# Attention with a gated MLP on one core: instructions recorded first and placed by a planner, chunk 0 by quarter tiles, early attention with tokens on partitions

## The chip, the core and the metric

The kernel runs on one core of a Trainium2 chip. Five engines take part, each with an instruction stream that it works through in order: TensorE (PE, with its weight loads as PEld), VectorE (DVE), ScalarE (ACT), GpSimd (POOL, hardly used here) and SyncE (SP), which issues the DMAs. Matmuls write to PSUM; everything else lives in SBUF or in DRAM. The metric is the device time of one launch in microseconds.

## The reference

```python
# x: 8 batches, 8 heads, 512 tokens, 64; state: 8 batches, 8 heads, 32 states, 64
scores = scale * x @ state.T;  a = softmax(scores)     # over the 32 states
xread  = a @ state                                     # 512 rows for each batch
scores2 = scale * state @ x.T; a2 = softmax(scores2)   # over the 512 tokens
sread  = a2 @ x                                        # 32 rows for each batch
X = concat([xread, sread]), heads side by side         # 4608 x 512
out = ((X @ w_a) * (X @ w_b)) @ w_out                  # 512 -> 1536 -> 512
```

All is float32.

## The kernel before

**Precision.** Float32 values are split into two parts of a shorter format, fp32r, high and low (`_h`, `_l`), and a product is made of three matmuls: high by high, low by high, high by low. The weights come as 64-bit words and are converted on the chip: class `Conv` loads one tile (`raw`), ScalarE scales it (`pre`), VectorE takes six operations of 512 columns (`run`), ScalarE writes the halves.

**Algebra.** xread is never formed. Since xread @ W = a @ (state @ W), the states are first multiplied into the weights. The 1536 columns of w_a and w_b are cut into six chunks (`c`) of 256 columns of each. For a chunk, `project` multiplies states (`sd_h`, `sd_l`) by weights (`wq`) for four batches at a time (`bg`), ScalarE copies the products to `sw_st` (or to `wo10`, `wo11`), and two DMAs for each pair of heads store them to DRAM (`scr`). `Batch.load` reads them back in another layout, one tile `p_raw` for a batch and a chunk, and `split` makes `p_h` (ScalarE) and `p_l` (VectorE). This store and load is called a round trip below, and the split tile a piece. Two pieces take a direct way (`DIRECT`): batch 0 with chunk 0 and batch 2 with chunk 1 get their products by small fp32 matmuls with the batch's own states (`direct`).

**Attention.** `Attention` handles one batch `b` and half of the heads `g`. `scores` puts states on partitions and tokens along the rows; `soft` takes the maxima over tokens, and VectorE's stream transpose turns 32x32 blocks so that the states lie along the rows for the other softmax (`s_p`); `exp`, `norm`; `back` turns the result again (`a_tr`) and splits it into `at_h`, `at_l`. `reads`, `sread` and `keep` make the 32 rows of sread with matmuls.

**MLP.** `layer1` of a step takes a batch and a block of 128 columns (`ft`): twice six matmuls of 512 columns from `p_h`, `p_l` and `at_h`, `at_l` into `ab`, then ScalarE copies, VectorE multiplies, and `g_h`, `g_l` are split. `layer2` of a step, which comes `LAG` = 2 steps later, adds twelve matmuls into `acc`. `VISITS` lists which batch takes which chunks, in order. A batch that comes back fetches its partial sums.

**Order.** The steps carry lists: `sp` and `pre` before layer 1, `fill` between the matmuls of layer 2, `post` behind it. Tables of step numbers (`ATTEND`, `CONV`, `CONVO`, `CONVS`) and a hand-written list `begin` say where each load, conversion, product and piece of attention goes. The framework's own scheduler then places the instructions within that.

Of the kernel before, what the change touches and what calls it, by code (L numbers as in the profile page):

```python
# [49 lines left out]
def attn_moe(ctx, tc, xt, xn, sd, wl, w_out, out):  # L50
    nc = tc.nc

    const = ctx.enter_context(tc.tile_pool(name="const", bufs=1))
    proj = ctx.enter_context(tc.tile_pool(name="proj", bufs=2))
    att = ctx.enter_context(tc.tile_pool(name="att", bufs=2))
    mlp = ctx.enter_context(tc.tile_pool(name="mlp", bufs=2))
    dram = ctx.enter_context(tc.tile_pool(name="dram", bufs=1, space=bass.MemoryType.DRAM))
    ps_acc = ctx.enter_context(tc.tile_pool(name="ps_acc", bufs=4, space=bass.MemoryType.PSUM))
    ps_ab = ctx.enter_context(tc.tile_pool(name="ps_ab", bufs=2, space=bass.MemoryType.PSUM))
    ps_ms = ctx.enter_context(tc.tile_pool(name="ps_ms", bufs=2, space=bass.MemoryType.PSUM))  # L60
# [7 lines left out]
    ident = const.tile([P, P], F32, name="ident")  # L68
    make_identity(nc, ident)
# [91 lines left out]
    def project(c, hp, bg, hh, psp, tag):  # L161
        if hh == 0:
            name, bufs = SW[st["n"] % len(SW)]
            st[bg], st["n"] = proj.tile([P, 2, 512], F32, name=name, bufs=bufs), st["n"] + 1
        sw = st[bg]
        ps = psp.tile([P, 512], F32, name=tag)
        for k, s in enumerate((sd_h, sd_l)):
            nc.tensor.matmul(ps, lhsT=s[hp // 2][:, 2 * (hp % 2) + hh, bg], rhs=w[c, hp][:, hh],  # L168
                             start=(k == 0), stop=(k == 1))
# [23 lines left out]
    class Attention:  # L193
# [5 lines left out]
        def load(self):  # L199
            self.x = att.tile([P, 2, S + D], F32, name="x_raw", bufs=1)  # L200
            nc.sync.dma_start(out=self.x, in_=xt[self.b, self.g])

        def scores(self):

            self.s = ps_ms.tile([P, 512], F32, name="ms")
            for hp in range(2):
                nc.tensor.matmul(self.s[hp * D:(hp + 1) * D], lhsT=self.x[:, hp, S:S + D],  # L207
                                 rhs=self.x[:, hp, :S], start=True, stop=True)

        def soft(self):  # L210
# [17 lines left out]
        def norm(self):  # L228
            sp, m1, m2 = self.sp, self.m1, self.m2
# [6 lines left out]
            nc.vector.tensor_scalar_add(out=m2[:, 3:4], in0=m2[:, 2:3], scalar1=EPS)  # L236
            nc.vector.reciprocal(out=m2[:, 3:4], in_=m2[:, 3:4])
# [8 lines left out]
        def reads(self):  # L246
            ps = ps_ms.tile([P, 512], F32, name="ms")
            for sb in range(4):
                nc.tensor.transpose(ps[:, sb * P:(sb + 1) * P], self.e2[:, sb * P:(sb + 1) * P], ident)  # L249
            self.a2 = att.tile([P, 4, P], F32, name="a2", bufs=1)  # L250
            nc.scalar.copy(out=self.a2.rearrange("p a b -> p (a b)"), in_=ps)
# [8 lines left out]
        def sread(self):  # L260

            ps = self.s = ps_ms.tile([P, 512], F32, name="ms")
            for sb in range(4):
                for hp in range(2):
                    nc.tensor.matmul(ps[hp * D:(hp + 1) * D, :P],  # L265
                                     lhsT=self.a2[:, sb, hp * D:(hp + 1) * D],
                                     rhs=self.xn[:, sb, hp * P:(hp + 1) * P],
                                     start=(sb == 0), stop=(sb == 3))
            nc.scalar.mul(out=self.a2[:, 0, :], in_=ps[:, :P], mul=self.m2[:, 3:4])
# [22 lines left out]
    class Batch:  # L292
# [20 lines left out]
        def direct(self, c, g, psp, tag, srcs):  # L313

            if g == 0:
                self.new_piece(c)
            ps = psp.tile([P, 512], F32, name=tag)
            for i, s in enumerate(srcs):
                for hq in range(4):
                    nc.tensor.matmul(ps[hq * NS:(hq + 1) * NS], lhsT=s(hq), rhs=f32(w[c, 2 * g + hq // 2][:, hq % 2]),  # L320
                                     start=(i == 0), stop=(i == len(srcs) - 1))
# [85 lines left out]

    def layer1(u, ft):
        res = []
        for ab in range(2):  # L410
            ps = ps_ab.tile([P, 512], F32, name="ab")
            m = 0
            for k in range(u.nk):
                xh, xl = u.rhs(k)
                wh, wlo = u.lhs(ft, k, ab)
                for a, b in ((wh, xh), (wh, xl), (wlo, xh)):
                    nc.tensor.matmul(ps[:, :u.n], lhsT=a, rhs=b, start=(m == 0), stop=(m == 3 * u.nk - 1))  # L417
# [11 lines left out]
    def layer2(u, ft, first, last, final, g, fill=()):  # L429
# [5 lines left out]
        for i in range(nt):  # L435
# [3 lines left out]
            for k, (l, r) in enumerate(((gh, 0), (gh, 1), (gl, 0))):  # L439
                nc.tensor.matmul(u.acc[i], lhsT=l[:, ts], rhs=wo[ft][:, r],  # L440
                                 start=(first and k == 0), stop=(last and k == 2))
# [10 lines left out]


    sp, pre, fill, post = ([[] for _ in steps] for _ in range(4))

    def at(where, n, f, *args):
        where[n].append(lambda: f(*args))

    queue = sorted([(n, 0, c, hp) for c, ns in CONV.items() for hp, n in enumerate(ns)] +
                   [(n, 1, ft, 0) for ft, n in CONVO.items()] +
                   [(n + j, 2, ft, j) for ft, n in CONVS.items() for j in range(2)])
    first = [(-1, 0, 0, hp) for hp in range(4)] + [(-1, 1, ft, 0) for ft in range(2)]
    queue = first + queue
    make = conv_w, lambda ft, _: conv_o(ft), units[SU].conv
    convs = [make[k](a, b) for _, k, a, b in queue]
    early = max(i for i, x in enumerate(queue) if x[0] < 35)
    late = min(i for i, x in enumerate(queue) if x[1] == 2)
    loads = []  # L470
    for i, c in enumerate(convs):
# [5 lines left out]
        loads.append((i + 1 - len(ring), c, ring[i % len(ring)]))
    done = [0]

    def next_load(n=1):  # L480

        done[0] += n
        while loads and loads[0][0] <= done[0]:
            _, c, place = loads.pop(0)
            c.load(place)
# [5 lines left out]


    a0, a1, a2 = [[atts[b, g] for g in range(2)] for b in range(3)]
    c0 = convs[:6]
    u0, u1, u2 = units[:3]

    def projects(c, hp, bg, psp=ps_acc, tag="acc"):
        for hh in range(2):
            project(c, hp, bg, hh, psp, tag)

    done[0] = -3
    begin = [next_load, a0[0].load, lambda: next_load(2), load_states, lambda: new_a(0),
             c0[0].pre, c0[0].run, a0[0].scores, next_load, a0[0].soft, a0[1].load, a0[0].nat,
             c0[1].pre, lambda: states(0, 0), c0[1].run, next_load, a0[0].exp, a0[0].norm, a0[1].scores,
             a1[0].load, c0[2].pre, lambda: u0.direct0(0, 0), a0[0].reads, a0[1].soft, a0[0].back,
             c0[2].run, next_load, lambda: states(1, 0), a0[1].exp, a0[1].norm, c0[3].pre,
# [136 lines left out]
```

## Time and profile before

| | |
|---|---|
| median of 3 runs | 756.52 us (756.07 to 756.76) |
| profiled execution | 758.62 us, of it span 756.8 us |
| TensorE busy | 711.0 us, 94% of the span |
| VectorE busy | 492.2 us, 65% |
| ScalarE busy | 392.6 us, 52% |
| mean granted clock of TensorE | 0.977 |
| moved by DMA | 134.30 MB, mean 177 GB/s |

Busy time counts an instruction from its start to its end; consecutive instructions of an engine overlap in their pipelines, so the distance of two starts is shorter than the duration of one. A row of a window gives, for each engine, the busy time and the number of instructions in it; an fp32 matmul leaves two records. The chain that ended last is followed back from the last instruction, at each step to what released it.

### The profile page before, as it was taken

How to read it: one execution, taken by the hardware profiler on the slowest of the kernel's cores; microseconds unless marked ns; L12 is line 12 of the kernel's file. 1: busy time of each engine (PE TensorE's matmuls, PEld its weight loads, DVE VectorE, ACT ScalarE, POOL GpSimd, SP SyncE). 2: the span in 40 equal slices, each digit the busy share in tenths (PEclk: the TensorE clock that was granted, in tenths of full speed). 3: DMA queues.
4: the chain of work that ended last, by engine and by line, in shares of the span. 5: the costliest groups of instructions: out<-in, count | busy, mean ns of one | idle time of the engine just before them, and what ended most of it. 6: DMA issues, size and time to landing. Idle time of an engine off the chain costs nothing.

```text
span 756.8 us, 9364 instructions
## 1 busy us (share of the span) xinstructions
PE 711.0 (94%) x3304; PEld 549.6 (73%) x3304; DVE 492.2 (65%) x961; ACT 392.6 (52%) x712; POOL 0.7 (0%) x6
## 2 busy tenths in 40 slices
PE   3759997999899999997999999999999999999997
PEld 0326765787577788885777777788889888888887
DVE  6989875887788754735899847463339823695232
ACT  5857848766786456755454424333236523553221
POOL 0000000000000000000000000000000000000000
PEclk9989999899899999998999999999999999999999
DMA  8795965947959573558888623121116311420002
GB/s 312 248 326 173 313 226 195 393 182 262 317 209 320 220 249 125 196 195 285 294 294 267 239 84 111 56 94 45 57 56 195 117 51 56 152 71 29 0 1 84
DMA packets 54798, 134.30 MB, mean 177 GB/s; under 512 B 5088, under 2 KB 5088, under 8 KB 54752
## 3 DMA queue, kind: packets, MB, share of 16 engines
q1 hardware_dynamic: 54464, 132.67, 50.7%
q10 hardware_dynamic: 288, 1.05, 0.4%
q8 instruction: 26, 0.43, 0.2%
q14 instruction: 20, 0.16, 0.1%
HBM read 87.03 MB, written 46.66 MB: 177 GB/s over the span
## 4 chain that ended last, share of the span: by engine, by line
PE 87%; DMA 5%; ACT 4%; DVE 2%; issue 1%; DVEq 0%; SPq 0%; ACTq 0%
PE ab L417 40%; PE acc L440 36%; PE ms L168 4%; PE ms L265 2%; DMA p_raw<-scr 2%; PE ms L207 2%; DMA scr<-wo 1%; PE ms L249 1%; DMA scr<-sw_st 1%; ACT wo L170 1%; DMA raw<-wl 1%; ACT sw_st L170 1%; ACT t L96 1%; DVE sd_l L66 1%; PE acc L320 1%
## 5 line engine op out<-in xcount | busy, mean ns | idle before, releaser
L440 PE MATMUL acc<-wo,g_h 128*128 128x512 f32 x816 | 232.8, 396 | 1.3 <-ACT g_h L425 1.3
L440 PEld LDWEIGHTS acc<-wo,g_h 128*128 128x128 f32 x816 | 151.9, 188 | 38.4 <-ACT g_h L425 1.7
L422 DVE TENSOR_TENSOR a_sb<-ab,a_sb 128x512 f32<-128x512 f32 (+1 forms) x108 | 71.3, 660 | 163.4 <-PE ab L417 158.2
L417 PE MATMUL ab<-at_h,p_h 128*128 128x512 f32 x384 | 157.0, 411 | 10.5 <-ACT at_h L243 5.5
L417 PE MATMUL ab<-at_l,p_h 128*128 128x512 f32 x384 | 155.2, 404 | 0.0
L417 PE MATMUL ab<-at_h,p_l 128*128 128x512 f32 x384 | 153.0, 401 | 0.0
L440 PE MATMUL acc<-wo,g_l 128*128 128x512 f32 x408 | 137.6, 398 | 0.0
L421 ACT COPY a_sb<-ab 128x512 f32<-128x512 f32 (+1 forms) x108 | 60.9, 564 | 140.7 <-PE ab L417 139.4
L425 ACT CAST g_h<-a_sb 128x512 fp32r<-128x512 f32 (+1 forms) x108 | 64.4, 596 | 72.6 <-DVE a_sb L422 72.3
L417 PEld LDWEIGHTS ab<-at_h,p_h 128*128 128x128 f32 x384 | 74.0, 193 | 35.7 <-ACT at_h L243 6.1
L440 PEld LDWEIGHTS acc<-wo,g_l 128*128 128x128 f32 x408 | 76.0, 188 | 18.8 <-DVE t L109 0.8
L417 PEld LDWEIGHTS ab<-at_l,p_h 128*128 128x128 f32 x384 | 74.6, 194 | 18.2 <-DVE m L236 1.6
L417 PEld LDWEIGHTS ab<-at_h,p_l 128*128 128x128 f32 x384 | 73.5, 192 | 18.1 <-DVE t L111 0.9
L66 DVE TENSOR_TENSOR g_l<-a_sb,g_h 128x512 fp32r<-128x512 f32 (+1 forms) x108 | 71.1, 658 | 22.7 <-ACT g_h L425 22.4
L310 ACT CAST p_h<-p_raw 128x512 fp32r<-128x512 f32 x92 | 52.4, 618 | 49.8 <-PE ab L417 40.3
L66 DVE TENSOR_TENSOR p_l<-p_raw,p_h 128x512 fp32r<-128x512 f32 x92 | 60.2, 683 | 7.5 <-ACT p_h L310 7.5
L102 DVE TENSOR_SCALAR t<-t 128x512 int32<-128x512 int32 x60 | 25.2, 423 | 31.0 <-ACT t L96 16.3
L168 PE MATMUL ms<-wq,sd_h 128*128 128x512 f32 x88 | 35.8, 407 | 4.9 <-ACT sw_st L170 4.6
L168 PE MATMUL ms<-wq,sd_l 128*128 128x512 f32 x88 | 35.1, 399 | 0.0
L170 ACT COPY sw_st<-ms 128x512 f32<-128x512 f32 x44 | 25.6, 589 | 15.3 <-PE ms L168 14.9
L207 PE MATMUL ms<-x_raw 128*64 128x512 f32 x64 | 19.2, 682 | 15.1 <-DMA x_raw<-xt 11.3
L170 ACT COPY wo<-ms 128x512 f32<-128x512 f32 x44 | 25.3, 589 | 11.0 <-PE ms L168 10.8
(98 smaller groups left out, 745.9 us busy)
## 6 DMA issues: line engine op xcount, KB each, us to landing
p_raw<-scr SPq DMA_DIRECT2D x46, 512.0 KB, 3.9
scr<-sw_st SPq DMA_DIRECT2D x48, 256.0 KB, 3.4
scr<-wo SPq DMA_DIRECT2D x48, 256.0 KB, 4.0
raw<-wl SPq DMA_DIRECT2D x21, 512.0 KB, 5.6
part<-stg SPq DMA_DIRECT2D x20, 512.0 KB, 4.1
stg<-part SPq DMA_DIRECT2D x20, 512.0 KB, 6.0
x_raw<-xt SPq DMA_DIRECT2D x16, 576.0 KB, 5.4
out<-stg SPq DMA_DIRECT2D x34, 256.0 KB, 3.8
```

The source lines that it names most:

```text
L66: eng.tensor_tensor(out=out, in0=in0, in1=in1, op=ALU.subtract)
L102: nc.vector.tensor_scalar(out=t2, in0=t1, scalar1=3, scalar2=0x7FFFF000, op0=ALU.logical_shift_left, op1=ALU.bitwise_and)
L168: nc.tensor.matmul(ps, lhsT=s[hp // 2][:, 2 * (hp % 2) + hh, bg], rhs=w[c, hp][:, hh], start=(k == 0), stop=(k == 1))
L170: nc.scalar.copy(out=sw[:, hh], in_=ps)
L207: nc.tensor.matmul(self.s[hp * D:(hp + 1) * D], lhsT=self.x[:, hp, S:S + D], rhs=self.x[:, hp, :S], start=True, stop=True)
L265: nc.tensor.matmul(ps[hp * D:(hp + 1) * D, :P], lhsT=self.a2[:, sb, hp * D:(hp + 1) * D], rhs=self.xn[:, sb, hp * P:(hp + 1) * P], start=( ...
L310: nc.scalar.copy(out=ph[:, g], in_=self.raw[c][:, g])
L417: nc.tensor.matmul(ps[:, :u.n], lhsT=a, rhs=b, start=(m == 0), stop=(m == 3 * u.nk - 1))
L421: nc.scalar.copy(out=g, in_=res[0][:, :u.n])
L422: nc.vector.tensor_tensor(out=g, in0=res[1][:, :u.n], in1=g, op=ALU.mult)
L425: nc.scalar.copy(out=gh, in_=g)
L440: nc.tensor.matmul(u.acc[i], lhsT=l[:, ts], rhs=wo[ft][:, r], start=(first and k == 0), stop=(last and k == 2))
```

## The change

The result is computed by the same algebra; three things differ.

**The order.** The tables, `begin` and the lists are gone. The code now runs once as a recording: `nc` is replaced by objects that note each engine call as a unit, with the 32-partition cells of the tiles that it reads and writes, and an estimated duration. The loop over `VISITS` writes units down in the order of need: attention of a batch, conversion and products of a chunk, loads, splits, layers. Each matmul of the MLP gets a due time (`paced`: estimated duration times 1.12, summed). `plan` derives dependences from cells and from the buffers of each pool, hands due times back through them, and then goes through a list schedule: at each step the engine that can start earliest takes, of its units that are ready then, the one with the earliest due time. PSUM tiles of `ms` are free to change order. The calls are then made in that order, under the framework's manual schedule.

**Chunk 0.** Its weights come as four tiles of one block of columns and four heads each (`weights(0, hp)`), in place of tiles of one head pair and both blocks. The direct products of batch 0 (`direct0`) are made for each block as soon as its tile is there, 256 columns at a time.

**Early attention.** For batches 0 and 1 (`WIDE`) the scores are made a second time with tokens on partitions (`scores_t`), and no stream transpose is made; the result goes back by TensorE transposes (`back_t`). For these and for `direct0`, the low part is made by `parts_of`: ScalarE writes the high part, a matmul by minus identity (`neg`, kept in `wo7`'s tile) subtracts it from the sum in PSUM, and ScalarE copies the rest out. The load of the states moves from ScalarE's DMA queue to SP's.

```diff
-ATTEND = {3: ((4, 9), (6, 10)), 4: ((16, 21), (19, 23)), 5: ((47, 51), (50, 54)),
...
-CONV = {1: (4, 4, 5, 5), 2: (8, 9, 10, 12), 3: (14, 15, 17, 18), 4: (26, 28, 29, 30), 5: (31, 32, 33, 34)}
...
+T0, PACE = 22e3, 1.12
+STARTS = {1: 25e3, 2: 45e3, 3: 65e3}
+WIDE = (0, 1)
...
+WAKE, SLACK = 500, 1.1
+def plan(units, pools, t0):
...
+    def parts_of(ps, h, l):
+        nc.scalar.copy(out=h, in_=ps)
+        nc.tensor.matmul(ps, lhsT=neg, rhs=h, start=False, stop=True, skip_group_check=True)
+        nc.scalar.copy(out=l, in_=ps)
...
+    def load_states(j):
+        raw = mlp.tile([P, 4, B * NS], F32, name="p_raw")
+        nc.sync.dma_start(out=raw, in_=sd[:, 4 * j:4 * j + 4])
...
+    def weights(c, hp):
+        if c:
+            return conv_w(wl[2 * c:2 * c + 2, :, hp, :].rearrange("f p x -> p f x"), c, hp)
+        f, g = hp // 2, hp % 2
+        return conv_w(wl[f, :, 2 * g:2 * g + 2, :], 0, f, g)
...
         def load(self):
-            self.x = att.tile([P, 2, S + D], F32, name="x_raw", bufs=1)
-            nc.sync.dma_start(out=self.x, in_=xt[self.b, self.g])
+            if self.g and self.b in WIDE:
+                self.x, t = [mlp.tile([P, 2, DM], F32, name="stg", bufs=4) for _ in range(2)]
+                self.st = t[:, :, :D]
+                nc.sync.dma_start(out=self.x, in_=xt[self.b, self.g, :, :, :S])
+                nc.sync.dma_start(out=self.st, in_=xt[self.b, self.g, :, :, S:])
...
+        def scores_t(self, psp, tag):
...
+                for sb in range(4):
+                    for hp in range(2):
+                        c = sb * P + hp * D
+                        nc.tensor.matmul(self.t[:, c:c + D], lhsT=self.x[:, hp, sb * P:(sb + 1) * P],
+                                         rhs=self.st[:, hp], start=True, stop=True)
+        def soft_t(self):
...
+            nc.vector.tensor_reduce(out=m1[:, 0, :], in_=t, axis=AX.X, op=ALU.max)
+            minus(nc.vector, sp, t, m1[:, 0, :].unsqueeze(2).broadcast_to([P, 16, 32]))
+        def back_t(self, psp, tag):
...
+                for sb in range(4):
+                    nc.tensor.matmul(ps[:, sb * P:(sb + 1) * P], lhsT=sp[:, sb * P:(sb + 1) * P], rhs=ident,
+                                     is_transpose=True, start=(sb == 0), stop=(sb == 3))
+            parts_of(ps, *(t[:, self.g, :] for t in a_t[self.b]))
...
+        def direct0(self, f, g):
...
+                for hq in range(4):
+                    x = hq // 2 * 256
+                    nc.tensor.matmul(ps[hq * NS:(hq + 1) * NS], lhsT=sd_raw[g][:, hq, n],
+                                     rhs=f32(w[0, f, g][:, hq % 2, x:x + 256]), start=True, stop=True)
+            parts_of(ps, *(t[:, g, f * 256:f * 256 + 256] for t in self.pieces[0]))
...
+    order, start = plan(rec.units, pools, T0)
+    with tc.manual_schedule():
+        for i in order:
+            for obj, method, args, kw in rec.units[i].calls:
+                getattr(obj, method)(*map(real, args), **{k: real(x) for k, x in kw.items()})
```

Since every call is now made at one place, all instructions of the changed kernel carry line 1047; its rows are told apart by their tiles.

TensorE at the start, before: the first products of chunk 0 (`acc<-wq,sd`) for four batches come ahead of layer 1 (`ab`).

```order
L207 MATMUL ms<-x_raw 64x512 x2
L320 MATMUL acc<-wq,p_raw 32x512 x2
L168 MATMUL acc<-wq,sd_h_83 128x512
L168 MATMUL acc<-wq,sd_l_85 128x512
L168 MATMUL acc<-wq,sd_h_83 128x512
L168 MATMUL acc<-wq,sd_l_85 128x512
L320 MATMUL acc<-wq,p_raw 32x512 x2
```

TensorE at the start, now; `wo_88` is the minus identity.

```order
L1047 MATMUL ms<-x_raw 128x64 x8
L1047 MATMUL ms<-x_raw 64x512 x2
L1047 MATMUL ms<-stg 128x64 x8
L1047 MATMUL acc<-wq,p_raw 32x256 x4
L1047 MATMUL ms<-ident,s_p 128x128 x4
L1047 MATMUL acc<-wq,p_raw 32x256 x4
L1047 MATMUL acc<-p_h,wo_88 128x256
L1047 MATMUL ms<-at_h,wo_88 128x512
L1047 MATMUL ab<-at_h,p_h 128x512
```

Layer 1 moves up to the ninth row: behind scores, direct products of the first block and one transposed tile of attention, and ahead of all products of chunk 0.

VectorE at the start, before: conversions of weights (`t`, `raw`, `wq`) and the states' low parts (`sd_l`) come first, the first maxima of attention 14th.

```order
L66 TENSOR_TENSOR sd_l_85<-p_raw,sd_h_83 128x4x4x32
L114 TENSOR_SCALAR raw<-t_137 128x512
L102 TENSOR_SCALAR t_171<-t_166 128x512
L116 SCALAR_TENSOR_TENSOR wq<-t_134,raw 128x512
L104 SCALAR_TENSOR_TENSOR t_171<-raw,t_171 128x512
L109 TENSOR_SCALAR t_166<-t_166 128x512
L66 TENSOR_TENSOR sd_l_86<-p_raw,sd_h_84 128x4x4x32 x2
L111 SCALAR_TENSOR_TENSOR t_166<-raw,t_166 128x512
L213 TENSOR_REDUCE m_152<-ms 128x1
L216 STREAM_TRANSPOSE s_p<-ms 128x512
```

VectorE at the start, now, its first ten rows.

```order
L1047 TENSOR_REDUCE m_124<-ms 128x16
L1047 TENSOR_TENSOR s_p<-ms,m_124 128x512
L1047 TENSOR_SCALAR t_130<-t_122 128x512
L1047 TENSOR_SCALAR t_122<-t_122 128x512
L1047 SCALAR_TENSOR_TENSOR t_130<-raw,t_130 128x512
L1047 SCALAR_TENSOR_TENSOR t_122<-raw,t_122 128x512
L1047 TENSOR_SCALAR raw<-t_130 128x512
L1047 SCALAR_TENSOR_TENSOR wq<-t_122,raw 128x512
L1047 TENSOR_SCALAR t_157<-t_140 128x512
L1047 TENSOR_REDUCE m_159<-ms 128x16
```

Attention's maxima and difference, taken straight from PSUM, now stand first; the stream transpose is gone, and the states' low parts move behind row 36.

TensorE where the first piece of chunk 5 that made a round trip is used, before: the last product of its four batches is the row ahead of these.

```order
L440 MATMUL acc<-wo_3069,g_h 128x512 x2
L440 MATMUL acc<-wo_3069,g_l 128x512
L440 MATMUL acc<-wo_3136,g_h 128x512 x8
L440 MATMUL acc<-wo_3136,g_l 128x512 x4
L168 MATMUL ms<-wq,sd_h_84 128x512
L168 MATMUL ms<-wq,sd_l_86 128x512
L168 MATMUL ms<-wq,sd_h_84 128x512
L168 MATMUL ms<-wq,sd_l_86 128x512
L207 MATMUL ms<-x_raw 64x512 x2
L417 MATMUL ab<-at_h,p_h 128x512
```

The same use now; the last product for this piece stands some fifty matmuls further up than the first row shown.

```order
L1047 MATMUL acc<-wo_2851,g_h 128x512 x2
L1047 MATMUL acc<-wo_2851,g_l 128x512
L1047 MATMUL ms<-wq,sd_h_211 128x512
L1047 MATMUL ms<-wq,sd_l_273 128x512
L1047 MATMUL ms<-wq,sd_h_211 128x512
L1047 MATMUL ms<-wq,sd_l_273 128x512
L1047 MATMUL ab<-at_h,p_h 128x512
```

Between the last product that a piece needs and its first use, other matmuls now stand in greater number: 19 matmuls and a pair of scores before, 58 matmuls now.

More of the change, by code (lines that the diff above doesn't have):

```diff
@@ L1 @@
[L1 removed]
+from contextlib import ExitStack, contextmanager
+import heapq
+import numpy as np
 import concourse.bass as bass
@@ L451, in attn_moe, with place, convert @@
         steps += [(units[u], ft, ft == fts[0], ft == fts[-1], final) for ft in fts]
[L454 to L471, printed above, removed]
+    def place(i, kind):
         ring = [("raw", 2)] * 2
-        if i <= early:
+        if kind == "early":
             ring += [(f"wo{ft}", 1) for ft in (8, 9)]
-        elif i >= late:
+        elif kind == "late":
             ring += [(f"sd_{x}{j}", 1) for x in "hl" for j in range(2)]
[L477 to L485, printed above, removed]
+        return ring[i % len(ring)]
+    count = [0]
+    def convert(c, kind):
+        c.load(place(count[0], kind))
+        count[0] += 1
+        c.pre()
+        c.run()
     def flush():
@@ L490, in flush @@
         nxt.clear()
[L493 to L506, printed above, removed]
-             lambda: projects(0, 0, 0), a0[0].sread, lambda: projects(0, 1, 0), a0[0].keep,
-             c0[3].run, next_load, flush, a0[1].back, lambda: u0.direct0(0, 1), a0[1].nat, a0[1].reads,
-             a1[0].scores, lambda: projects(0, 2, 0), lambda: projects(0, 3, 0), flush,
-             a1[0].soft, c0[4].pre, lambda: states(0, 1), lambda: states(1, 1)]
@@ new lines, in products @@
+    def products(c, bg, where=ms):
+        for hp in range(4):
+            for hh in range(2):
+                project(c, hp, bg, hh, *where)
+        flush()
+    for j in range(2):
+        load_states(j)
+    new_a(0)
+    for f in range(2):
+        for g in range(NG):
+            convert(weights(0, 2 * f + g), "early")
+            units[0].direct0(f, g)
+    attend(0)
+    for j in range(2):
+        states(j, 0)
+    products(0, 0, acc)
+    for ft in range(2):
+        convert(conv_o(ft), "early")
@@ new lines, in attn_moe, with chunk @@
+    for j in range(2):
+        states(j, 1)
+    products(0, 1)
+    made, ready = {0}, {0}
+    def chunk(c):
+        if c in made:
+            return
+        made.add(c)
+        for hp in range(4):
+            convert(weights(c, hp), "early" if c < 5 else "")
+        for u, d in DIRECT:
+            if d == c:
+                for g in range(NG):
+                    units[u].direct1(c, g)
+        for bg in range(2):
+            products(c, bg)
+        for ft in (2 * c, 2 * c + 1):
+            convert(conv_o(ft), "early" if c < 4 else "")
```

609 lines of the change are left out of this document (468 added, 141 removed).

## Prediction

> **What bounds the kernel now.** I read the page's totals and its chain first, then busy time by stage, then the chain in order of time where the stages lose.
>
> ```profile
> span 756.8 us, 9364 instructions
> PE 711.0 (94%) x3304; PEld 549.6 (73%) x3304; DVE 492.2 (65%) x961; ACT 392.6 (52%) x712; POOL 0.7 (0%) x6
> PE 87%; DMA 5%; ACT 4%; DVE 2%; issue 1%; DVEq 0%; SPq 0%; ACTq 0%
> ```
>
> TensorE makes 87% of the chain that ended last, so the time is its work plus what it loses. Where it loses shows in the windows (PE, PEld, DVE, ACT and POOL busy with counts, granted clock, DMA share, GB/s):
>
> ```profile
> 0.00:50.00 50.00, 25.68 (x121) 11.08 (x121) 39.77 (x88) 32.76 (x56) 0.70 (x6) 0.99 0.82 284
> 50.00:100.00 50.00, 45.51 (x214) 30.56 (x215) 46.08 (x103) 38.59 (x73) 0.00 (x0) 0.87 0.79 268
> 100.00:134.00 34.00, 29.45 (x130) 21.42 (x129) 19.68 (x39) 21.78 (x41) 0.00 (x0) 0.96 0.57 201
> 134.00:198.00 64.00, 61.15 (x274) 46.23 (x272) 51.15 (x100) 43.05 (x77) 0.00 (x0) 0.95 0.75 273
> 500.00:700.00 200.00, 200.00 (x956) 166.50 (x955) 113.89 (x209) 81.42 (x148) 0.00 (x0) 1.00 0.27 85
> ```
>
> From 500 us on TensorE never stops. In the first 50 us it does 121 records, half the late pace (956 in 200 us), while VectorE is busy 40 us and then 46 of 50. The start is the place to gain; the late part has nothing to give.
>
> The steady prices, from the late chain and from the early timeline at full clock:
>
> ```profile
> 512.19 2.79 PE acc L440 x12
> 565.19 2.87 PE ab L417 x24
> 25.70 1.08 PE L207 MATMUL ms<-x_raw 128*64 128x512 f32 x4
> 26.71 0.66 PE L249 MATMUL ms<-ident,e 128*128 128x128 f32 x4
> 28.10 1.05 PE L320 MATMUL acc<-wq,p_raw 128*32 128x512 f32 x4 [0.73 <-ACT wq L121]
> 30.23 1.09 PE L265 MATMUL ms<-x_nat,a 128*64 128x128 f32 x16
> ```
>
> A 512-column fp32r matmul is 2.79/12 = 0.2325 us, a 256-column one 0.119; a pair of scores 1.0 (start to start), four transposes 0.66, a set of sreads 1.09, four direct products 0.98. With the counts of the program these make 685 us of TensorE work before, so about 72 us are lost. I cut the span at the first use of reloaded pieces, which both kernels have in the same sequence of visits: R0 (chunk 0), R1 (chunk 1), R2 (chunk 2), R5 (chunk 5). The chain there:
>
> ```profile
> 38.73 4.92 DMA scr<-wo
> 43.70 6.03 DMA p_raw<-scr
> 56.77 2.01 PE ab L417 x4
> 133.61 4.27 PE ab L417 x10
> 187.42 0.47 PE ms L168 x2
> 188.53 2.77 DMA scr<-sw_st
> 191.36 6.11 DMA p_raw<-scr
> 198.17 4.63 PE ab L417 x10
> 341.33 3.99 DMA scr<-wo
> 346.59 5.05 DMA scr<-sw_st
> 351.69 3.36 DMA p_raw<-scr
> 355.75 2.08 PE ab L417 x4
> ```
>
> So the stages before are: to R0 56.8 us for 26.0 us of TensorE work (counted in the order at the prices above), R0 to R1 76.8 for 59.3, R1 to R2 64.6 for 58.3, R2 to R5 157.6 for 150.3, R5 to the end 401.0 for 391.0. Losses: 30.8, 17.5, 6.3, 7.3 and 10.0. At R2 a product goes out at 187.4 and comes back as a piece at 198.2, a round trip of 10.8 us with only 6.5 us of other TensorE work placed inside. At R5 it is worse: a second store waits behind a load on SP's queue, and 338 to 355.7 makes 17.
>
> **The change part by part.** *Arithmetic on TensorE, added:* four groups (batches 0 and 1) get transposed scores, 4 sets of eight, at 1.1 us as the sread row (between 0.66 of the transpose row and 2), four sets of transposes at 0.66, and eight matmuls by minus identity (4 x 0.2325 + 4 x 0.119): 4.4 + 2.6 + 1.4 = 8.4 us. Total 693.3. All lies ahead of R1.
>
> *VectorE, relieved.* Removed: 8 stream transposes, 4 differences of at_l, 2 of p_l; the maxima now read PSUM at the same count. Ahead of R1 stand 184 VectorE instructions against 225 in the order before. The three first windows have 230 of them in 105.5 us, 0.459 each: 184 make 84 us, plus 6.5 of start 91. ScalarE there: 170 in 93.1, 0.548 each, and 144 ahead of R1 make 79 (8 new low-part copies are among them). Neither reaches the time that TensorE needs to R1 (87.4 of work plus the start's loss), so VectorE stops setting the pace.
>
> *To R0.* The chain is new. ScalarE's first work waits for the first landing and matmuls began thus:
>
> ```profile
> 5.88 0.66 ACT L96 ACTIVATE t<-raw 128x512 f32<-128x512 f32 x1 [2.93 <-DMA raw<-wl]
> 6.44 2.04 ACT L142 CAST sd_h<-p_raw 128x512 fp32r<-128x512 f32 x2
> 12.41 0.45 DVE L109 TENSOR_SCALAR t<-t 128x512 int32<-128x512 int32 x1
> 12.74 2.12 DVE L66 TENSOR_TENSOR sd_l<-p_raw,sd_h 128x512 fp32r<-128x512 f32 x2
> 14.74 0.72 DVE L111 SCALAR_TENSOR_TENSOR t<-raw,t 128x512 f32<-128x512 uint32 x1
> 15.35 0.72 DVE L213 TENSOR_REDUCE m<-ms 128x1 f32<-128x512 f32 x1
> 35.12 0.73 PE L417 MATMUL ab<-at_h,p_h 128*128 128x512 f32 x2
> L107 ACT CAST wq<-t 64x512 fp32r<-64x512 f32 x24 | 14.8, 617 | 0.6
> ```
>
> Now x_raw is issued first and the first tile of weights second; with the first landing at 5.9 and the scores at the slow early clock I put the first maxima at 7.5. VectorE's rows 1 to 20 (two conversions of three instructions at 0.61 and three at 0.33 us each, start to start by the VectorE rows above; two maxima and two differences at 0.61; one norm of four instructions, two of them short, about 1.5) are 9.6 us plus hand-offs: the first attention tile is done near 18.5, through TensorE and ScalarE near 20, and layer 1 starts there instead of at 35.1. From then ScalarE has 35 instructions (its rows 18 to 52: weight halves at 0.62, states at 1.02, the rest, I estimate, near 0.5) to the last copy of chunk 0's products, 19.6 us, with 2.5 us of waits 42; 65 instructions at 0.548 from 6 us give 41.6, the same. Store and load by the rows above take 2.8 to 4.9 and 3.4 to 6.1 us, the split 0.6: 10.5. R0 comes at 52.5 with 30.1 us of TensorE work done, of which 12.8 lie inside that round trip. 4 us earlier, 4 us more done.
>
> *R0 to R1:* 57.3 us of work, and a loss of 5. What remains there is the clock after a wait:
>
> ```profile
> 47.00:50.00 3.00, 0.00 (x0) 0.00 (x0) 1.31 (x2) 0.25 (x1) 0.00 (x0) 0.92 0.98 322
> 50.00:53.00 3.00, 0.98 (x2) 0.50 (x2) 2.57 (x6) 2.05 (x5) 0.00 (x0) 0.50 1.03 406
> 56.00:59.00 3.00, 3.00 (x7) 1.84 (x6) 3.00 (x9) 2.48 (x5) 0.00 (x0) 0.50 0.91 287
> 198.00:202.00 4.00, 3.83 (x9) 3.06 (x10) 3.46 (x7) 3.93 (x8) 0.00 (x0) 0.50 1.05 406
> 30.00:40.00 10.00, 8.50 (x62) 4.87 (x60) 9.62 (x24) 8.73 (x18) 0.00 (x0) 1.00 0.92 332
> 90.00:100.00 10.00, 10.00 (x51) 6.05 (x50) 9.69 (x22) 7.16 (x14) 0.00 (x0) 1.00 0.93 295
> ```
>
> After an idle stretch the granted clock stays at half for 4 us (from 198) to 9 us (50 to 59), which costs 2 to 4.5. I take 3 for R0 and 2 for hand-offs (bounds 0, and the 17.5 of before). [...]
>
> *R1 to R2:* 58.4 of work. R1's round trip has 13.6 us of other work inside (before 9.3), so its wait shrinks to 0 to 1; R2's has 7.9 (before 6.5), a wait of 3 against 4.3. With a short half clock I take 4 (bounds 1 and 6.3). *R2 to R5:* 152.7; R5's has 13.7 inside (before 5.7), two reloads for batch 4 now fall here with 13.9 and 12.5: loss 3.5 (bounds 1.5 and 7.3). *R5 to end:* 394.8; of the 10.0 lost, 2.3 were the half clock behind R5, and about 4 are the last store; 7.5 stay.
>
> *Queues.* The states' load moves from ACT's queue to SP, behind seven loads; two x loads are split, 2 more issues. Both lie inside the 20 us above. The order of SP's stores is the plan's; 70 DMAs stand ahead of R1 (75 before), 29.8 MB against 33.6. At the 309 GB/s that I estimate from busy windows (above: 332, 295) that is 96 us, under the 115 that the sum gives, so transfers are covered; without that cover each late MB costs 3 us.
>
> *Sum:* 52.5 + 62.3 + 62.4 + 156.2 + 402.3 = 735.7 us of span. The profiled execution took 758.62 for a span of 756.8, and the median of the runs is 756.52, 0.3 below the span: I predict 735.4.
>
> **Rivals.** *The engines pack better (720).* R0 bound by bytes alone: 13.4 MB at 309 GB/s, 43 us and 3 of start, 46; losses then 2, 1, 2 and 6.5: 46 + 59.3 + 59.4 + 154.7 + 401.3 = 720.7. For it: the bounds are all below. Against: in no early window do three engines run full. [...]
>
> *Half the gain is lost in hand-offs (750).* The early rows now pass many small tiles ScalarE, TensorE, ScalarE, and ScalarE has become as loaded as VectorE. With R0 at 57 as before, 12 us lost to R1, 7 to R2, 6 and 8.5 after: 57 + 69.3 + 65.4 + 158.7 + 403.3 = 753.7; with one of these as forecast, 748 to 750. For it: before, R0 to R1 lost 17.5. Against: VectorE then was 92% busy, and now has 24 us of slack.
>
> *Slower by round trips (760).* The order is fixed by estimated durations. Eight reloads have less than 17.3 us of work inside (12.8, 13.6, 7.9, 15.1, 17.0, 13.9, 12.5, 13.7). If each took the 17 us seen at R5 the shortfall is 32 us, about 24 beyond the sum: 760. It decides from a mean round trip near 16 us. R2 with 10.8 is against, and what made R5 slow, a store behind a load that waited for VectorE, is one queue order.
>
> *No change.* The built order differs from the first row on, so the change does what it says; only losses that happen to balance would give it.
>
> **How the numbers follow.** Forecast (726 to 746) 0.58, better packing 0.13, half the gain 0.14, slower 0.10, no change 0.05. Faster is 0.85. 0.2% (1.5 us) is about what a measurement can tell from no change. The range reaches from the packed case to the half-gain case, 719 to 752; the forecast's own is 726 to 746.
>
> **What would show it.** Right: layer 1's first matmul near 20 us; R0 near 52, R1 near 115, R2 near 177; VectorE's busy share below 90% in 50 to 100 us; TensorE's records in the first 100 us up from 335 to about 470; the two stores and the load at 341 to 355 gone from the chain. Wrong: waits of TensorE for p_h of 5 us or more at several reloads, a clock of 0.5 in more than two stretches, or waits of TensorE for ScalarE's casts that sum to over 15 us in the first 100.

## The result and the profile after

The changed kernel takes 734.87 us (median of 4 runs, 734.07 to 738.54) against 756.64 for the kernel before on the same chip: a ratio of 0.972, 95% interval 0.968 to 0.976, or 21.8 us less. The profiled execution took 734.27 us. From its page, the span, the busy times and the chain that ended last by engine:

```profile
span 732.5 us, 9629 instructions
PE 706.2 (96%) x3440; PEld 557.7 (76%) x3440; DVE 495.8 (68%) x947; ACT 394.9 (54%) x723; POOL 0.7 (0%) x6
PE 92%; ACT 5%; DMA 1%; DVE 1%; issue 1%; DVEq 0%; SPq 0%; ACTq 0%
```

TensorE is busy 4.8 us less although 8.4 us of work were added (counted at the prediction's prices); its mean clock rose from 0.977 to 0.997. Its idle time (span less busy) fell from 45.8 to 26.3 us. Three windows as before the change (PE, PEld, DVE, ACT, POOL busy with counts, clock, DMA share, GB/s):

```profile
0.00:50.00 50.00, 38.94 (x217) 28.79 (x218) 38.04 (x76) 34.65 (x63) 0.70 (x6) 1.00 0.71 258
50.00:100.00 50.00, 42.30 (x240) 27.61 (x243) 38.77 (x86) 37.10 (x71) 0.00 (x0) 1.00 0.77 273
198.00:356.00 158.00, 158.00 (x720) 125.50 (x720) 107.55 (x199) 98.92 (x179) 0.00 (x0) 1.00 0.70 248
```

In the first 100 us TensorE has 457 records in place of 335, VectorE falls from 46 to 39 of 50 us in the second window, and from 198 us on TensorE does not stop. The cuts R0, R1, R2 and R5 are read here from the trace of each kernel as the 9th, 33rd, 65th and 153rd matmul `ab<-at_h,p_h`, which use the same piece of the same batch in all of them. From the timelines, before and then after:

```profile
35.12 0.73 PE L417 MATMUL ab<-at_h,p_h 128*128 128x512 f32 x2
64.43 0.50 PE L417 MATMUL ab<-at_h,p_h 128*128 128x512 f32 x1
133.26 0.77 PE L417 MATMUL ab<-at_h,p_h 128*128 128x512 f32 x1
```

```profile
22.43 0.63 PE L1047 MATMUL ab<-at_h,p_h 128*128 128x512 f32 x1
54.60 0.50 PE L1047 MATMUL ab<-at_h,p_h 128*128 128x512 f32 x1 [1.31 <-ACT p_h L1047]
120.08 0.39 PE L1047 MATMUL ab<-at_h,p_h 128*128 128x512 f32 x1
336.50 0.40 PE L1047 MATMUL ab<-at_h,p_h 128*128 128x512 f32 x1
```

With the prediction's counts of TensorE work (before 26.0, 59.3, 58.3, 150.3 and 391.0 us by stage; after 30.1, 57.3, 58.4, 152.7 and 394.8), stage length less work gives the time that TensorE lost:

| stage | before: us, lost | after: us, lost | predicted lost |
|---|---|---|---|
| start to R0 | 64.4, 38.4 | 54.6, 24.5 | 22.4 |
| R0 to R1 | 68.9, 9.6 | 65.5, 8.2 | 5 |
| R1 to R2 | 64.9, 6.6 | 62.8, 4.4 | 4 |
| R2 to R5 | 157.5, 7.2 | 153.6, 0.9 | 3.5 |
| R5 to end | 401.1, 10.1 | 396.0, 1.2 | 7.5 |
| sum | 71.9 | 39.2 | 42.4 |

So, by these counts, TensorE lost 13.9 us less at the start, 15.2 less behind R2, and 3.6 less in between. TensorE's remaining waits after (total, times, longest), and what its windows show where it still loses:

```profile
PE ms L1047 <- DVE s_p L1047: 4.5, 1, 4.5
PE ms L1047 <- DMA x_raw<-xt: 4.3, 1, 4.3
PE ms L1047 <- ACT wo L1047: 3.9, 2, 2.4
PE ab L1047 <- ACT p_h L1047: 1.7, 2, 1.3
```

```profile
80.00:90.00 10.00, 7.47 (x37) 5.43 (x37) 8.63 (x19) 9.46 (x18) 0.00 (x0) 1.00 1.00 346
90.00:100.00 10.00, 8.34 (x47) 4.59 (x49) 7.98 (x16) 9.72 (x18) 0.00 (x0) 1.00 0.73 267
182.00:184.00 2.00, 1.57 (x6) 0.96 (x5) 1.63 (x4) 1.95 (x4) 0.00 (x0) 0.65 1.03 386
184.00:186.00 2.00, 2.00 (x6) 1.61 (x5) 1.49 (x4) 1.98 (x5) 0.00 (x0) 0.50 1.03 417
186.00:188.00 2.00, 2.00 (x10) 1.60 (x9) 1.90 (x5) 1.95 (x5) 0.00 (x0) 1.00 1.03 394
```

The two long waits lie in the first 24 us. From 80 to 100 us ScalarE is the full engine, 19.2 of 20 us busy. At R2 it is full again, and the chain there goes through its queue: the copies of the products and the piece's cast stand behind casts of weights.

```profile
175.79 0.47 PE ms L1047 x2
...
176.94 0.62 ACT wq L1047
...
179.34 0.66 ACT t L1047
...
180.66 1.07 ACT wo L1047 x2
...
182.26 0.63 ACT p_h L1047
...
182.94 4.44 PE ab L1047 x12
```

### The profile page after: what moved, and what is told of

The parts are those of the page before. It is cut to its first block, busy times and chain, and to the rows that moved or that the text cites. A ratio compares the mean times of both kernels' runs of the same rounds, so it can differ in the third digit from the quotient of the medians.

```text
span 732.5 us, 9629 instructions
## 1 busy us (share of the span) xinstructions
PE 706.2 (96%) x3440; PEld 557.7 (76%) x3440; DVE 495.8 (68%) x947; ACT 394.9 (54%) x723; POOL 0.7 (0%) x6
## 3 DMA queue, kind: packets, MB, share of 16 engines
q1 hardware_dynamic: 55040, 133.71, 52.5%
## 4 chain that ended last, share of the span: by engine, by line
PE 92%; ACT 5%; DMA 1%; DVE 1%; issue 1%; DVEq 0%; SPq 0%; ACTq 0%
PE ab L1047 40%; PE acc L1047 39%; PE ms L1047 13%; ACT wq L1047 2%; DMA p_raw<-scr 1%; DMA x_raw<-xt 0%; ACT stg L1047 0%; ACT t L1047 0%; ACT wo L1047 0%; ACT p_h L1047 0%; ACT sd_h L1047 0%; ACT e L1047 0%; DVE m L1047 0%; ACT sw_st L1047 0%; ACT at_h L1047 0%
## 5 line engine op out<-in xcount | busy, mean ns | idle before, releaser
L1047 PE MATMUL acc<-wo,g_h 128*128 128x512 f32 x816 | 259.3, 397 | 0.1
L1047 PE MATMUL acc<-wo,g_l 128*128 128x512 f32 x408 | 159.3, 396 | 0.0
L1047 PE MATMUL ab<-at_h,p_h 128*128 128x512 f32 x384 | 152.4, 400 | 1.9 <-ACT p_h L1047 1.7
L1047 PE MATMUL ab<-at_l,p_h 128*128 128x512 f32 x384 | 152.2, 397 | 0.0
L1047 PE MATMUL ab<-at_h,p_l 128*128 128x512 f32 x384 | 150.8, 396 | 0.0
L1047 PEld LDWEIGHTS ab<-at_h,p_h 128*128 128x128 f32 x384 | 73.0, 190 | 22.4 <-ACT p_h L1047 3.6
L1047 DVE TENSOR_TENSOR g_l<-a_sb,g_h 128x512 fp32r<-128x512 f32 (+1 forms) x108 | 70.8, 655 | 20.9 <-ACT g_h L1047 20.8
L1047 ACT CAST p_h<-p_raw 128x512 fp32r<-128x512 f32 x92 | 52.8, 619 | 13.8 <-PE ab L1047 9.3
L1047 DVE TENSOR_SCALAR t<-t 128x512 int32<-128x512 int32 x120 | 49.8, 422 | 9.6 <-ACT t L1047 8.5
L1047 PE MATMUL ms<-wq,sd_h 128*128 128x512 f32 (+2 forms) x112 | 38.8, 418 | 7.3 <-ACT wo L1047 3.9
L1047 ACT CAST wq<-t 64x512 fp32r<-64x512 f32 (+1 forms) x64 | 39.4, 619 | 8.2 <-PE ms L1047 2.9
L1047 DVE SCALAR_TENSOR_TENSOR t<-raw,t 128x512 int32<-128x512 int32 (+1 forms) x60 | 39.7, 686 | 0.3
L1047 PE MATMUL ms<-wq,sd_l 128*128 128x512 f32 (+2 forms) x112 | 37.7, 406 | 0.0
```

The source lines that it names most:

```text
L1047: getattr(obj, method)(*map(real, args), **{k: real(x) for k, x in kw.items()})
```

## The experiments

Two explanations stood against each other. *Theory A:* the order found by the plan brings the gain. *Theory B:* the arithmetic that relieves VectorE brings it. The table gives the starts of the cuts in the profiled execution, the median time and the ratio to the kernel before on the same chip (the runs were made on several chips); the edits follow. No run has the new arithmetic in the order of the kernel before, and none undoes the move of the states' load alone.

| kernel | first layer 1 | R0 | R1 | R2 | R5 | us | ratio (interval) |
|---|---|---|---|---|---|---|---|
| before | 35.1 | 64.4 | 133.3 | 198.2 | 355.7 | 756.6 | 1 |
| changed | 22.4 | 54.6 | 120.1 | 182.9 | 336.5 | 734.9 | 0.972 (0.968 to 0.976) |
| e1_narrow | 20.4 | 54.0 | 119.2 | 185.1 | 338.5 | 736.5 | 0.973 (0.971 to 0.975) |
| e2_dve_low | 21.6 | 53.7 | 125.0 | 193.5 | 348.1 | 745.4 | 0.985 (0.983 to 0.986) |
| e3_whole | 32.2 | 54.5 | 118.9 | 181.8 | 335.0 | 734.1 | 0.970 (0.968 to 0.971) |
| e4_plan_only | 27.9 | 56.8 | 125.6 | 188.2 | 345.9 | 743.5 | 0.982 (0.980 to 0.984) |
| e8_same_order | 21.5 | 53.5 | 123.1 | 186.0 | 339.5 | 736.9 | 0.974 (0.971 to 0.978) |
| e9_other_order | 21.9 | 54.5 | 126.7 | 195.5 | 349.7 | 746.2 | 0.987 (0.983 to 0.991) |
| e5_no_due | 39.2 | 70.8 | 126.3 | 200.2 | 362.8 | 777.0 | 1.029 (1.025 to 1.032) |
| e6_framework | 26.0 | 55.3 | 134.0 | 191.1 | 351.2 | 760.9 | 1.007 (1.004 to 1.010) |
| e10_plan_only_108 | 28.1 | 56.5 | 124.8 | 185.5 | 339.1 | 739.9 | 0.980 (0.978 to 0.981) |
| e11_pace_120 | 22.4 | 55.9 | 122.3 | 183.7 | 336.5 | 745.1 | 0.987 (0.984 to 0.989) |
| e12_starts | 22.2 | 53.1 | 118.7 | 179.9 | 334.5 | 733.1 | 0.971 (0.969 to 0.972) |
| e13_whole_one | 33.7 | 53.4 | 119.4 | 178.6 | 333.0 | 732.2 | 0.970 (0.968 to 0.971) |

**One part of the arithmetic undone at a time.** In each of the next four the plan runs anew and finds its own order.

```diff
-WIDE = (0, 1)
+WIDE = ()
```

> All attention is done with states on partitions and stream transposes, as before; order by the plan, chunk 0 by quarter tiles and the minus identity for the direct products stay. TensorE has 7.9 us less work (685.4 for 693.3), all ahead of R1; VectorE's work ahead of R1 rises from 79 to 87 us. Theory A (the order brings the gain, because layer 1 starts early and the round trips are covered): 731 to 740 us, first layer-1 matmul before 26 us. Theory B (relief of VectorE brings it): the start falls back to VectorE's pace, first layer-1 matmul after 30 us, 745 us or more.

736.5 us, the first matmul of layer 1 at 20.4 us: theory A's range. TensorE has 7.9 us less to do (at the prediction's prices) and the median is 1.6 us higher, so that it loses 9.5 us more: about 7 ahead of R1 and 3 between R1 and R2. Alone, the wide attention makes no difference that these runs can tell.

```diff
-        nc.tensor.matmul(ps, lhsT=neg, rhs=h, start=False, stop=True, skip_group_check=True)
-        nc.scalar.copy(out=l, in_=ps)
+        minus(nc.vector, l, ps, f32(h))
```

> Low parts of the transposed attention and of the direct products are made by VectorE's subtraction from PSUM, as before, not by the minus identity and a second ScalarE copy; the rest is the changed kernel. TensorE 1.4 us less, ScalarE about 4.6 less and VectorE about 3.5 more, all ahead of R1. Theory A: 733 to 737 us; if ScalarE is what holds up 80 to 100 us, then 732 or 733. Theory B: VectorE is back in the way, 738 to 742 us.

745.4 us, worse than either theory allowed. But of the 10.5 us, 4.9 arise ahead of R1 and 5.7 between R1 and R2, where no low part of this kind is made: suspicion falls on the new order (taken up below).

```diff
-    for f in range(2):
-        for g in range(NG):
-            convert(weights(0, 2 * f + g), "early")
-            units[0].direct0(f, g)
+    for g in range(NG):
+        for i in range(2):
+            convert(weights(0, 2 * g + i), "early")
+        units[0].direct0(g)
```

> Chunk 0 comes by tiles of one pair of heads and both blocks, as before, and its direct products wait for two tiles each; the rest is the changed kernel. Layer 1 then needs four conversions in place of two ahead of it (VectorE 17.8 us of work ahead of it for 9.5, ScalarE 19.2 for 10.4). Theory A: first layer-1 matmul near 29 us for 22.4; the work put off falls into the wait before R0 only in part: 737 to 742 us. Rival (chunk 0's tiles don't matter, since R0 is set by ScalarE's copies of the products and those need all four tiles anyway): R0 within 1 us of 54.6 and 734 to 736 us.

The rival holds. From the timeline of e3_whole, the first layer 1 and R0:

```profile
32.16 0.62 PE L1038 MATMUL ab<-at_h,p_h 128*128 128x512 f32 x2
54.48 0.50 PE L1038 MATMUL ab<-at_h,p_h 128*128 128x512 f32 x1
```

Layer 1 starts 9.7 us later than in the changed kernel, R0 comes at the same time, and the kernel takes 734.1 us. So the early first matmul, conspicuous as it is, does not bring R0 forward, and the kernel without the quarter tiles is no slower. The order was planned anew here too; a worth of the tiles in one and the same order is not shown.

Next, e4_plan_only, all three of these edits together:

> The plan's order alone: attention, low parts and the tiles of chunk 0 as before. TensorE's work is that of the kernel before (684.9 us). Theory A: the order brings more than half of the 22 us, 734 to 744 us, and R1, R2, R5 come within 6 us of the changed kernel's. Theory B (the arithmetic edits bring most): 746 us or more, with the first layer-1 matmul near 35 us and R1 near 130 us as before. If the edits and the order each only work together, about 756.

743.5 us: the order with the former arithmetic brings 13.8 of the 22 us (0.982). R1 and R2 are within 6 us of the changed kernel's; R5, 9.4 behind, is not.

**Order or arithmetic: both exchanged.** e2_dve_low changed both at once, the low parts and, since the plan ran anew, the order. The next kernel keeps the changed kernel's order and exchanges the arithmetic when the calls are issued.

```diff
+                if kw.get("lhsT") is neg:
+                    continue
+                if id(call) in low:
+                    minus(base.vector, real(kw["out"]), real(kw["in_"]), f32(low[id(call)]).real())
+                    continue
```

> The order of the changed kernel is kept call for call; only where it is issued, each of the eight products by minus identity is left out and the ScalarE copy behind it is replaced by VectorE's subtraction from PSUM. So this is e2_dve_low's arithmetic in the changed kernel's order (e2_dve_low let the plan run anew and took 745.4 us). Theory O (e2_dve_low lost its 10 us to the order that the plan then found, with the products for R2 placed 10 us later): 733 to 738 us, R2's first cast within 2 us of 182.3. Theory V (VectorE must be kept free of the low parts): 741 us or more.

The other one takes e2_dve_low's order and issues a matmul by minus identity and a ScalarE copy for each subtraction.

```diff
+                if id(call) in low:
+                    ps, h = real(kw["in0"]), real(low[id(call)])
+                    base.tensor.matmul(ps, lhsT=real(neg), rhs=h, start=False, stop=True, skip_group_check=True)
+                    base.scalar.copy(out=real(kw["out"]), in_=ps)
+                    continue
```

> The reverse: the order that the plan found for e2_dve_low, but issued with the arithmetic of the changed kernel (minus identity and ScalarE copy). Theory O: 743 to 747 us, R2's first cast after 190 us. Theory V: 733 to 738 us.

736.9 and 746.2 us: the time goes with the order, not with the arithmetic. Only R2's cast in e8_same_order missed its bound, 3.1 us late for 2. By the timelines of both, the last pair of products for R2's piece starts at 175.7 us in e8_same_order and at 180.0 in e9_other_order, its store has landed at 180.5 and 184.9, and the load that fetches it is issued at 180.6 and 187.4. The chains show the cast, in e9_other_order the load too:

```profile
185.34 0.63 ACT p_h L1056
```

```profile
187.36 7.43 DMA p_raw<-scr
...
194.82 0.63 ACT p_h L1055
```

In e9_other_order the last pair comes 4.4 us later; then the load stands for 2.4 us behind two stores of other products in SP's queue, and it takes 7.4 us for 3.9. It lies bare in the chain, which in e8_same_order goes through ScalarE's queue. (In e2_dve_low itself the last pair for R2 starts at 178.3 us for 172.6 in the changed kernel, 5.7 us later and not 10.)

**The plan itself.** Now the arithmetic stays that of the changed kernel.

```diff
-        late[i] = d
+        late[i] = float(i)
```

> The plan's list schedule stays, but among ready units the one written first goes first, not the one due first; arithmetic as in the changed kernel. Work ahead of R0, R1 and R2 on TensorE rises by 5 to 6 us and on ScalarE by 13, 11 and 5 us. Theory A (the due times are what brings layer 1 forward and covers the round trips): first layer-1 matmul after 32 us and 750 to 775 us, the whole gain or more lost. Rival C (any list schedule that fills the engines does it): 733 to 742 us.

777.0 us: 42 us over the changed kernel and 20 over the kernel before, 2 beyond the range. A list schedule that always keeps its engines fed is not enough. In its chain a round trip lies open; a product ends at 325.2 and comes back at 341.5, and the last pair for that piece, which the chain passes by, ends at 328.2, 13.3 us ahead of the cast:

```profile
324.75 0.47 PE ms L1047 x2
...
329.28 3.80 DMA scr<-wo
...
333.23 8.23 DMA p_raw<-scr
...
341.48 0.63 ACT p_h L1047
```

Round trips are not all of it. In the profiled executions 18 of the 45 us by which its span is longer arise behind R5, where no transfer stands in its chain: between 571 and 592 us TensorE waits 10.7 us, the longest time (4.4 us) for attention's `e`, and the granted clock is 0.50 from 578 to 591 us (0.97 on the mean of 500 to 700).

```diff
-    with tc.manual_schedule():
-        for i in order:
+    for i in order:
```

> The calls are made in the plan's order, but without the manual schedule: the framework's scheduler may place them anew. Ahead of the first layer-1 matmul stand then 13.9 us of VectorE's work for 9.5 and 14.4 of ScalarE's for 10.4; at R1 and R2 the work ahead is within 2 us of the changed kernel's. Theory A (the exact order counts, mainly at the start and at R2): 738 to 748 us. Rival (written in the right order, the framework keeps what matters): 733 to 737 us.

760.9 us, outside both ranges and slower than before: the framework's scheduler, given the calls in the planned order, loses 26 us. At the first layer 1 and R0 it is 3.6 and 0.7 us behind, at R1 13.9 us, at R5 14.7; the loss behind R5 stays open. At R1 its chain has a bare round trip that the changed kernel's chain does not have:

```profile
123.01 2.36 DMA scr<-wo
...
125.50 7.83 DMA p_raw<-scr
...
133.35 0.63 ACT p_h L1046
```

**How much is the list's luck.** Two kernels change one number of the plan.

```diff
-T0, PACE = 22e3, 1.12      # e4_plan_only
+T0, PACE = 22e3, 1.08      # e10_plan_only_108
```

> The kernel of e4_plan_only (arithmetic and tiles as before, 743.5 us) with one number of the plan changed, the pace of the due times from 1.12 to 1.08. The list that the plan then writes ends at 734.2 us by its own durations, 738.6 in e4_plan_only and 729.2 in the changed kernel; on the chip the six planned kernels ran 1.6 to 8.5 us, on the mean 5, beyond their lists. Theory O (what looked like the worth of the arithmetic edits was in part the order that the plan happened to find): 736 to 741 us. Theory W (the edits are worth the 8.6 us by which e4_plan_only is behind the changed kernel): 742 us or more.

739.9 us. With a better list the former arithmetic is 5 us behind the changed kernel and 6.9 behind the better list for the same new arithmetic (e12_starts). Against the changed kernel, that rest lies ahead of R1: e10_plan_only_108 reaches R1 4.7 us later, R5 only 2.6 later. The comparison favours the new arithmetic: e12_starts is the best of some 190 lists, and of the former arithmetic two lists were run. Whether a still better list would take the rest away is not shown.

```diff
-T0, PACE = 22e3, 1.12      # the changed kernel
+T0, PACE = 22e3, 1.2       # e11_pace_120
```

> The changed kernel with the pace 1.20 in place of 1.12 and nothing else: the same instructions, due times more stretched. Its list ends at 739.9 us, 10.7 later than the changed kernel's. Theory O (the order alone moves the time by 10 us): 742 to 748 us. Rival (the engines take up such shifts, since each works as soon as its inputs are there): 734 to 738 us.

745.1 us, as the order theory has it: 10 us for one number, with the same instructions. R5 is reached at the same time; the loss lies behind it, 13.3 us in the profiled execution, which was the slowest of its five runs (747.75). TensorE's waits behind R5 make 4.8 us of it, and a granted clock of 0.50 from 384.5 to 391.3 us 3.4; the rest stays open. There the chain leaves TensorE and goes through VectorE's queue, where the partial sums that a returning batch closes (`stg`), conversions (`t`, `wq`) and attention (`m`, `s_p`) have all been put ahead of the next piece:

```profile
365.49 2.78 PE ab L1047 x12
...
369.43 1.04 DVE t L1047 x2
...
374.60 0.68 DVE stg L1047
...
379.25 0.70 DVE m L1047
...
382.60 2.17 ACT p_h L1047 x4
...
385.54 6.59 PE ab L1047 x16
```

**Better lists.** Two kernels from a search over the plan's numbers:

```diff
-T0, PACE = 22e3, 1.12
-STARTS = {1: 25e3, 2: 45e3, 3: 65e3}
+T0, PACE = 22e3, 1.1
+STARTS = {1: 25e3, 2: 55e3, 3: 65e3}
```

> The changed kernel with the pace 1.10 and the second visit's earliest due time at 55 us for 45: the best list found among some 190 settings, end 727.2 us for 729.2. If the list's end holds to 2 us, 731 to 735 us; if the differences between good lists are lost in what the list doesn't know of the chip, 734 to 739 us.

The second builds on e3_whole:

```diff
-T0, PACE = 22e3, 1.12
-STARTS = {1: 25e3, 2: 45e3, 3: 65e3}
-WIDE = (0, 1)
+T0, PACE = 22e3, 1.09
+STARTS = {1: 25e3, 2: 40e3, 3: 70e3}
+WIDE = (0,)
```

> Chunk 0 by tiles of a pair of heads and both blocks (as in e3_whole), the wide attention for batch 0 only, pace 1.09, earliest due times 25, 40 and 70 us: 4.0 us less work on TensorE than the changed kernel, list's end 727.8 us. If the least work with a good list wins: 730 to 734 us. If VectorE's 5 us more ahead of R1 hold it up, 735 to 740 us.

733.1 and 732.2 us, both in the first of their ranges. R2 moves from 182.9 to 179.9 and 178.6. The medians are 1.8 and 2.7 us below the changed kernel's, but the intervals of the ratios overlap: not slower, and not shown to be faster. The lower of them does with half of the wide attention and without quarter tiles.

## Why the prediction was right, and where it was not

Predicted 735.4, measured 734.9. The total owes something to errors that cancel: the cuts came 2.1 (R0), 5.3 (R1), 5.7 (R2) and 3.1 us (R5) late, the span's end 3.2 early. That the two totals are only 0.5 us apart is therefore in part luck.

*R0 of before was misread.* The prediction took the row at 56.77 for the first use of a reloaded piece. It is the rest of batch 0's first step, whose second half of attention was late; batch 1's first use is at 64.43. Its piece had been cast at 49.75, 14.7 us ahead of that:

```profile
49.75 0.63 ACT p_h L310
52.02 1.22 PE L417 MATMUL ab<-at_h,p_h 128*128 128x512 f32 x2 [5.52 <-ACT at_h L243]
```

So the round trip did not bound R0 before; batch 0's own step did. In the changed kernel the load of that piece is issued later (47.90 for 43.70), and R0 comes earlier all the same, because batch 0's step is done by then. The work of 26.0 us had been counted to the right place. So R0 came 9.8 us earlier, not 4; the loss before was 38.4 to R0 and 9.6 (not 17.5) from there to R1. The step "R0 to R1", for which the prediction promised 12.5 us of gain, brought 1.4, and the start brought 13.9 where 8.4 were promised. The sum of both, 15.3, was nearer, 20.9 promised.

*To R0: 52.5 said, 54.6 measured.* The path of the changed kernel was as argued: ScalarE's copies of chunk 0's products, store, load, split. From the last copy on it took 10.0 us for 10.5 said. The last copy was late: it ends at 44.6 us for 42 said, and ScalarE waited for TensorE's products ahead of it. In SP's queue the load then stood behind one of `x_nat`, which waited 2.1 us for TensorE:

```profile
43.97 0.59 ACT L1047 COPY wo<-acc 128x512 f32<-128x512 f32 x1 [1.11 <-PE acc L1047]
47.32 0.34 SPq L1047 DMA_DIRECT2D x_nat<-xn  x1
47.90 6.01 DMA p_raw<-scr
```

The mis-sized term on TensorE's side is the transposed scores, 1.1 us for a set of eight. In the changed kernel's timeline a set takes 1.89 (1.71 to the next start), and about twice that at the start (two records for each matmul; the first group also holds the pair of scores behind the set):

```profile
4.31 5.58 PE L1047 MATMUL ms<-x_raw 128*128 128x64 f32 x20 [4.31 <-DMA x_raw<-xt]
10.06 3.65 PE L1047 MATMUL ms<-stg 128*128 128x64 f32 x16 [0.16 <-PE ms L1047]
26.73 0.63 PE L1047 MATMUL ab<-at_l,p_h 128*128 128x512 f32 x1
33.37 1.89 PE L1047 MATMUL ms<-x_raw 128*128 128x64 f32 x16
35.39 0.39 PE L1047 MATMUL ab<-at_l,p_h 128*128 128x512 f32 x1
```

For the four sets that is 2.4 us of work more than counted, all ahead of R0. How much of the 2.1 us is theirs stays open: e1_narrow, which has none of them and an order of its own, reaches R0 only 0.6 us earlier. The half pace at the start lasts beyond the scores: up to 28 us matmuls of 512 columns start 0.43 us apart, later 0.23. All this put the first layer 1 at 22.4 for 20, which e3_whole shows to be without consequence for R0.

*R0 to R1: a loss of 5 said, 8.2 measured, and of another kind.* The 3 us for the clock did not arise: between 50 and 100 us the granted clock was 1.00; why that stretch was spared, no row tells. In e1_narrow, where TensorE waited 5.3 us for `p_h` at R0, the clock was 0.50 from 53 to 59 us (0.86 on the mean of 50 to 100); that the term fell away in the changed kernel, and so offset part of what follows, was luck. The other 2 us, for hand-offs, were too few: ScalarE was full from 80 to 100. The prediction had summed ScalarE's work ahead of R1 to 79 us and found it below TensorE's 87.4, and passed over that it bunches. The only half-clock stretch that the granted clock still shows is at R2: the windows at 182 and 184 us make 0.7 x 2 + 2 = 3.4 us at half. Of the 9 us at 50 to 59 before, TensorE was idle up to 52.0 and for 0.5 us ahead of 53.75; then it worked for 5.7 us, to 59.4, and was at half all the while.

*R1 to R2:* 4 said, 4.4 measured. The chain at 176 to 182 us goes through ScalarE's queue, and TensorE waited 2.4 us there for the copies of products. But the piece itself was held by that queue for 0.9 us only: its load was issued at 177.5 and landed 3.9 us later, and the cast began at 182.26. So the round trip, as predicted, was nearly as late as ScalarE. *R2 to R5:* 3.5 said, 0.9 measured: all reloads there are covered, the two moved ones too. Before, TensorE had waited for the cast at R5 itself:

```profile
PE ab L417 <- ACT p_h L310: 2.4, 1, 2.4
```

*R5 to end:* 7.5 said, 1.2 measured. The prediction let all stay but the half clock (2.3 us), which is gone: the granted clock is 1.00 from 336 us to the end. The last store stays too: TensorE's work in the chain ends 4.2 us ahead of the span's end (before: 4.4). A loss of 1.2 us, less than these 4.2, says that the work is priced too high for the changed kernel. One price did change: twelve matmuls of layer 1 take 2.79 us in the chain before and 2.73 now (layer 2's take 2.79 in both).

```profile
514.99 2.79 PE ab L417 x12
365.71 2.73 PE ab L1047 x12
```

Behind R5 stand 58 such groups, by which I estimate up to 3.5 us, and up to 5.8 of the 21.8 us over the 96 groups of the whole kernel. The chain of e6_framework has 2.75 (at 117.29 us), so the exact order does not explain it; what does is open, and the prediction has no term for it. For the other 2.8 us or more no row was found.

*VectorE* fell to 78% from 50 to 100 us, as said. That this relief is what frees the start is not borne out: undone singly, the edits cost 1.6 (wide attention), 2.0 (low parts, same order) and -0.8 us (tiles), none of it measurable; undone together 8.6, or 5 to 7 with a better list. Whether the edits bring this in company, or a list that suits the former arithmetic as well was not found, is left open. Shown is that the planned kernel with the former arithmetic has 13.8 to 15.4 us of the gain, and that eight low parts do not matter in a fixed order.

*The rivals.* "Slower by round trips" had its price wrong. The 17 us at R5 before were counted from 338, but the last product for that piece ends at 345.5 in the timeline, about 10 us ahead of the first use at 355.75; at R2's 10.8 as price, seven of the eight reloads that the prediction lists have work enough inside, all but R2's own. e5_no_due is slower than before and has a round trip of 13.3 us, but loses much behind R5 for other reasons. "Half the gain lost in hand-offs" is in time roughly e2_dve_low, e9_other_order and e11_pace_120 (745 to 746), the last of them one plan number away. That R0 follows the bytes (46) is out: the first 50 us moved 258 GB/s.

## What to carry to other kernels

When a planner sets the order, an edit of the arithmetic runs the planner anew, and the order that it then happens to find can cost more than the edit (here 10 us against 2): exchange arithmetic under a fixed order before believing a comparison. Compare such kernels each with a few settings of the plan, and look for the stage in which the time differs; if nothing was edited there, suspect the order. An engine's summed work ahead of a point says little: look in 10 us windows for where it bunches, and count a stage from the same instruction in both kernels.

## What was unexpected of the hardware

Eight fp32 matmuls of 64 columns over 128 rows took 1.89 us at full clock, and 3.65 in the first 14 us of the launch although the granted clock shows 1.00 there too; a pair of 512 columns over 64 rows takes 1.08. The half pace lasted through 9.4 us of almost unbroken work of TensorE (4.3 to 13.7) and, after a pause, up to 28 us. The load of one piece took 3.2 to 8.9 us from issue to landing in the kernel before, with a median of 3.9; the three bare loads shown above (7.4 to 8.2) are among the long ones.
